# Spectrum by rows: the second transform of a long FFT as two constant 64 by 64 weights, in a kernel that filters and routes tokens

## The chip, the cores and the metric

The kernel runs on one core of a Trainium2 chip. The metric is the device time of one execution in microseconds (us). The kernel before takes 374.61 us, the median of three runs that lie between 374.57 and 374.65 us.

The engines are PE (TensorE matmuls; PEld is its weight load), DVE (VectorE), ACT (ScalarE), POOL (GpSimd) and SP, which here only issues DMAs. Matmul results land in PSUM; only DVE and ACT read it in this kernel.

## The reference

The input `x` is (8, 2496, 256) in fp32: 8 batches of 2496 tokens of 256 channels. Per channel a circular convolution runs over the tokens, as an FFT, a product with a filter spectrum and an inverse FFT:

```
X = rfft(x, axis=1);  Y = X * (filt_r + 1j * filt_i);  y = irfft(Y)         # (8, 2496, 256)
logits = y @ phi                                   # all 19968 tokens, 32 slots
d = softmax(logits over tokens);   slot_in  = d.T @ y                        # (32, 256)
slot_out = relu(slot_in @ w1[e]) @ w2[e]           # 8 experts with 4 slots each
c = softmax(logits over slots);    out = c @ slot_out
```

The output is (19968, 256) in fp32.

## The kernel before, in words

2496 is 39 times 64, which have no common factor, so a token has two indices (`s` below 39, `k` below 64) and the transform is one over 39 followed by one over 64. Since the input is real, 20 frequencies `t` of the first transform are kept. The filtered tokens are never formed: logits and the weighted sum over tokens are both taken in the spectrum.

**Batches and slots.** A batch has 10 slots of two `t` each; the main loop runs over 80 slots, `n` = 0 to 79. The first transform of batch `b+1` is made while batch `b` goes through its slots, in six units `u` of 512 elements a partition (the one with `u` = 0 has half).

**A unit of the first transform.** SP loads `xt` from HBM (`load_x`, six buffers). `fold_x` adds and subtracts the tokens `s` and 39-`s`: two ops on POOL (lines L334 and L337). `s1_unit` (L355) makes four matmuls of 64 rows by 64 columns, one on each quarter of PE, 512 columns wide, with the constant `w1q`. ACT copies the result to `at` (L364), and `store_a` stores it to the HBM scratch `a_dram`. `load_ash` reads it back with the 64 `k` (real and imaginary part) on the 128 partitions. Batch 0 has a way of its own (`first_stage`, `turn`) and is not stored.

**A slot.** `x_unit` (L433) makes the second transform with the DATA as weights: four matmuls with 128x128 blocks of `ash` as weights and 128 columns of a constant as the moving operand. Out comes the spectrum with channels on partitions and frequencies along the row, in `ps_x`, a PSUM pool of two buffers of one bank. DVE multiplies it by the filter: `t2` = spectrum (parts swapped) times the filter's imaginary part (L453), spectrum times the real part in place (L455), one sum and one difference into `yt` (L456, L457). From batch 6 on (`PA`) the last two run on POOL. `t_unit` (L465) transposes `yt` (four 128x128), and ACT copies this to `y`, frequencies on partitions, which is kept for the weighted sum. Every second slot `l_unit` (L492) multiplies `phi` with `yt`: the logits' spectrum.

**The chains.** When a group of batches (two, two, two, one, one) is through its slots, its `chain` takes the logits' spectrum back to tokens (`ltr`, `v`, `lg`), takes the maximum and the exponential (`d`), transforms that (`u`, `u2`, `dd`) and sums `dd` times `y` (`s`). A chain is a generator in steps; two steps go into each slot (`hop_slot`). DVE makes its PSUM copies, maxima and differences.

**After the loop** come the last chain steps, the experts, and the output (`combine`, `blocks`: L1100, L1105), stored through `ob`.

**What sets the order.** Each engine works in order through a list that the framework makes: it simulates the program and lets each engine take the instruction that is ready first and of the highest priority. Chosen edges without a wait (`not_before`, `behind`) fix PE's order in a slot and all early DMA issues on SP. So the order of a list may differ from that of the source, and a wait for a semaphore holds up everything behind it on its engine.

Of the kernel before, what the change touches and what calls it, by code (L numbers as in the profile page):

```python
# [205 lines left out]
def token_layout(x):  # L206

    rows = np.zeros((len(x), 2, 64, NH, 2, DIM), x.dtype)
    for u in range(NH):
        for k in range(PK * 2 * u, min(PK * 2 * (u + 1), N2)):  # L210
            r, j = divmod(k - PK * 2 * u, PK)
            for s in range(HR):
                rows[:, r, HR * j + s, u, 0] = x[:, token_of(s, k)]
                if s:
                    rows[:, r, HR * j + s, u, 1] = x[:, token_of(N1 - s, k)]
    return rows.reshape(len(x), P, NI, DIM)
# [36 lines left out]
def fft_soft_moe(ctx, tc, x0, w0, x, ff, phi, wx, cst, w1q, sgn, out):  # L253
# [73 lines left out]
    def fold_x(b, u):  # L327

        lo, hi = PIECE[u]
        n = hi - lo  # L330
# [3 lines left out]
        ins = eng.tensor_tensor(out=eo[:, 0, 0:n], in0=xs[:, :, 0], in1=xs[:, :, 1], op=ALU.add)  # L334
# [2 lines left out]
        ins = eng.tensor_tensor(out=eo[:, 1, 0:n], in0=xs[:, :, 0], in1=xs[:, :, 1], op=ALU.subtract)  # L337
# [6 lines left out]
    def s1_unit(b, u, floor=None):  # L344
        if u == 0:
            a_dram[b] = scr.tile([2, N2, NT, DIM], F32, tag="a_dram", name=f"a_dram{b}")
        lo, hi = PIECE[u]
        n = hi - lo
        eo = eos.pop((b, u))
        both = ps_s1[0].tile([P, 2, 2, DIM], F32, tag="s1", name=f"s1_{b}_{u}")  # L350
        with tc.high_priority():
            for c, r in ((1, 0), (1, 1), (0, 0), (0, 1)):
                q = slice(64 * r, 64 * r + 64)
                ps = both[64 * c : 64 * c + 64, r, 0:n]
                ins = pe.matmul(ps, w1q_t[q, c], eo[q, c, 0:n], start=True, stop=True)  # L355
# [8 lines left out]
        act.copy(at[:, 0:n], both[:, :, 0:n].rearrange("q r u d -> q u r d"))  # L364
# [25 lines left out]
    def load_ash(b, c):  # L390
        t0 = 2 * c
        ash = prod.tile([P, 2, DIM], F32, tag="ash", name=f"ash{b}_{c}", bufs=ASH)
        ashs[b, c] = ash
        issue(ash, a_dram[b].rearrange("r k t d -> (r k) t d")[:, t0 : t0 + 2, :])
# [756 lines left out]
```

## Time and profile before

| | |
|---|---|
| median of three runs | 374.61 us |
| the profiled execution's own time | 377.61 us |
| its span, first to last instruction | 375.8 us |
| PE busy | 345.0 us, 92% of the span |
| DVE busy | 262.4 us, 70% |
| ACT busy | 175.8 us, 47% |
| POOL busy | 149.1 us, 40% |
| bytes moved by DMA | 104.17 MB, mean 277 GB/s |
| granted TensorE clock, mean | 0.951 |
| main loop (slots 0 to 79) | 16.9 to about 276 us of the span |

The stretch up to 16.9 us loads the first tokens and makes batch 0's first transform; that behind 276 us holds the last chain steps, the experts (about 302 to 319 us) and the output. The profile's page gives shares over the whole span; its view by windows cuts these into stages, and a restriction to one line (L433) shows where a batch begins, since each batch has 80 instructions of that line (each fp32 matmul is two).

### The profile page before, as it was taken

Reading aid. Unit: us, or ns where it says so; the run is one execution under the profiler, and the core shown is the slowest. Engines: PE = TensorE matmul, PEld = TensorE weight load, DVE = VectorE, ACT = ScalarE, POOL = GpSimd, SP = SyncE. Lnnn points to the kernel's source line nnn. Section 1 sums busy time; section 2 is a strip of 40 time slices with the busy share of each in tenths; the row PEclk is TensorE's granted clock in tenths of the full one; section 3 lists DMA queues with packets and bytes.
Section 4 is the critical chain, followed back from the end, with each engine's and each line's share of the span. In section 5 each row is a group of like instructions: output and inputs, shape, how many; then the busy total and the mean of one; then the engine's idle time right before and its main releaser. Section 6 shows DMA issues by size and latency. Waiting matters only on the chain. (4 is left out here: it accounts for less than half of the span.)

```text
span 375.8 us, 10512 instructions
## 1 busy us (share of the span) xinstructions
PE 345.0 (92%) x4254; PEld 257.5 (69%) x4254; DVE 262.4 (70%) x519; ACT 175.8 (47%) x354; POOL 149.1 (40%) x180
## 2 busy tenths in 40 slices
PE   8998989899998899999889998899989999999960
PEld 6865767578676567777566775777867635879960
DVE  2555878796998869689996857685674552786650
ACT  3474545445556244646534544534363430765540
POOL 0189638536348204644640664333531302650000
PEclk9999999999999999999999999999999999995555
DMA  8999899699699549969953757642897993599996
GB/s 301 396 394 352 246 332 360 213 335 384 216 367 337 175 110 317 323 211 297 320 176 102 200 167 219 248 139 60 271 364 227 363 298 82 238 415 413 415 419 285
DMA packets 50438, 104.17 MB, mean 277 GB/s; under 512 B 5250, under 2 KB 23810, under 8 KB 48214
## 3 DMA queue, kind: packets, MB, share of 16 engines
q1 hardware_dynamic: 49700, 103.16, 78.8%
q8 instruction: 33, 0.54, 0.6%
q10 hardware_dynamic: 690, 0.35, 0.3%
q14 instruction: 15, 0.12, 0.1%
HBM read 63.37 MB, written 40.12 MB: 275 GB/s over the span
## 5 line engine op out<-in xcount | busy, mean ns | idle before, releaser
L433 PE MATMUL x<-cst_t,ash 128*128 128x128 f32 x640 | 85.7, 276 | 3.1 <-DMA ash<-a_dram 3.1
L453 DVE TENSOR_TENSOR t<-x,ff_t 128x512 f32<-128x512 f32 x80 | 55.2, 690 | 45.2 <-PE x L433 29.4
L334 POOL TENSOR_TENSOR eo<-xt 128x512 f32<-128x512 f32 (+1 forms) x40 | 49.0, 1225 | 94.4 <-issue 86.4
L433 PEld LDWEIGHTS x<-cst_t,ash 128*128 128x128 f32 x640 | 78.1, 192 | 5.3 <-DMA ash<-a_dram 3.8
L364 ACT COPY at<-s 128x1024 f32<-128x1024 f32 (+1 forms) x42 | 39.6, 943 | 50.0 <-PE s L355 33.2
L465 PE MATMUL t<-cst_t,yt 128*128 128x128 f32 x320 | 49.9, 278 | 0.0
L337 POOL TENSOR_TENSOR eo<-xt 128x512 f32<-128x512 f32 (+1 forms) x40 | 48.5, 1212 | 0.0
L479 ACT COPY y<-t 128x512 f32<-128x512 f32 x58 | 33.8, 587 | 30.8 <-PE t L465 30.6
L355 PE MATMUL s<-eo,w1q_t 64*64 64x512 f32 (+1 forms) x336 | 42.8, 579 | 4.6 <-POOL eo L337 4.4
L455 DVE TENSOR_TENSOR x<-x,ff_t 128x512 f32<-128x512 f32 x60 | 41.8, 696 | 1.3
L465 PEld LDWEIGHTS t<-cst_t,yt 128*128 128x128 f32 x320 | 36.0, 141 | 9.5 <-issue 5.6
L1100 PE MATMUL out<-so,st 32*128 32x256 f32 x468 | 36.0, 367 | 1.1 <-DVE ob L1105 0.9
L1100 PEld LDWEIGHTS out<-so,st 32*128 32x128 f32 x468 | 32.7, 253 | 3.6 <-DVE ob L1105 1.7
L492 PEld LDWEIGHTS l<-yt,phi_t 128*32 128x32 f32 x640 | 15.2, 109 | 25.9 <-issue 20.7
L1105 DVE COPY ob<-out 128x512 f32<-128x512 f32 (+1 forms) x40 | 25.2, 672 | 8.5 <-PE out L1100 7.8
L456 POOL TENSOR_TENSOR yt<-yt,t 128x256 f32<-128x256 f32 x20 | 15.1, 754 | 35.0 <-DVE yt L455 25.3
L1105 ACT COPY ob<-out 128x512 f32<-128x512 f32 (+1 forms) x40 | 21.9, 581 | 14.0 <-PE out L1100 11.4
L456 DVE TENSOR_TENSOR yt<-x,t 128x256 f32<-128x256 f32 x60 | 25.2, 421 | 1.3
L492 PE MATMUL l<-yt,phi_t 128*32 128x128 f32 x640 | 25.7, 278 | 0.0
L457 DVE TENSOR_TENSOR yt<-x,t 128x256 f32<-128x256 f32 x60 | 24.9, 415 | 0.0
L526 PE MATMUL s<-y,dd 128*32 128x256 f32 x232 | 19.2, 381 | 0.3 <-ACT dd L680 0.3
L479 ACT COPY yb<-t 128x512 f32<-128x512 f32 x20 | 11.7, 586 | 10.7 <-PE t L465 10.7
(117 smaller groups left out, 481.9 us busy)
## 6 DMA issues: line engine op xcount, KB each, us to landing
xt<-in_x SPq DMA_DIRECT2D x35, 512.0 KB
ash<-a_dram SPq DMA_DIRECT2D x70, 256.0 KB
out<-ob SPq DMA_DIRECT2D x17, 1024.0 KB
a_dram<-at SPq DMA_DIRECT2D x56, 240.0 KB
w<-in_wx SPq DMA_DIRECT2D x33, 256.0 KB
w<-in_wx SPq DMA_DIRECT2D x6, 512.0 KB
x_t<-in_x SPq DMA_DIRECT2D x5, 512.0 KB
ff_t<-in_ff SPq DMA_DIRECT2D x10, 256.0 KB
```

What stands on the lines that cost most here:

```text
L334: ins = eng.tensor_tensor(out=eo[:, 0, 0:n], in0=xs[:, :, 0], in1=xs[:, :, 1], op=ALU.add)
L337: ins = eng.tensor_tensor(out=eo[:, 1, 0:n], in0=xs[:, :, 0], in1=xs[:, :, 1], op=ALU.subtract)
L355: ins = pe.matmul(ps, w1q_t[q, c], eo[q, c, 0:n], start=True, stop=True)
L433: ins = pe.matmul(ps[:, 2 * k + dh].rearrange("q r c -> q (r c)"), ash[:, k, dh * P : (dh + 1) * P], C("a1" if t0 + k else "b0"), start=Tr ...
L453: dve.tensor_tensor(out=t2, in0=ps[:, :, ::-1, :], in1=fiv, op=ALU.mult)
L455: dve.tensor_tensor(out=part, in0=ps, in1=frv, op=ALU.mult)
L456: add.tensor_tensor(out=yt[:, :, 1, :], in0=part[:, :, 1, :], in1=t2[:, :, 1, :], op=ALU.add)
L465: ins = pe.transpose(pt[:, k, dh, :], yt[:, c % 2, 2 * k + dh].rearrange("q r c -> q (r c)"), ident)
L479: act.copy(y, pt.rearrange("k p h d -> k p (h d)"))
L492: ins = pe.matmul(pl[32 * j : 32 * j + 32, :], phi_t[:, dh, :], yt[:, j // 2, 2 * (j % 2) + dh].rearrange("q r c -> q (r c)"), start=(dh = ...
L1100: nc.tensor.matmul(prs[k][:, mm, :], sts[n][q, hs, c0 : c0 + P], so[q, ho], start=(i == 0), stop=(i == 2))
L1105: copy(ob[:, nm * k : nm * (k + 1), :], prs[k])
```

## The change

**The tokens are folded over both indices.** The 64 `k` are folded too: of `k` and 64-`k` the sum and the difference are formed before the first transform. `fold_x` therefore has four ops in place of two: sum and difference over `k` into a scratch tile `eo` (one buffer, `EB`), then sum and difference over `s` back into `xt`. All four have 512 elements a row (256 for `u` = 0). The second of the four runs on DVE (`FD = (1,)`), the others on POOL; for the first two units all run on DVE. `xt` is read by the matmul itself, so it comes free when `s1_unit` is done, not when the fold is done. The load of the next `xt` is issued behind that unit's store (`next_x` in `store_a`).

**The second transform has constant weights.** A slot pair (four `t`) has one `x_pair`: four matmuls of 64 by 64, one on each quarter of PE, 512 columns wide, with the constants `xf` and `xf0` as weights and `ash` as the moving operand (six matmuls for the pair that holds `t` = 0). Batch 0, which is not folded over `k`, has 128 rows by 64 columns. The spectrum stands in rows: frequencies on partitions, channels along the row. That is the layout of `y`, so DVE's product goes to `y` directly, with 1024 and 512 elements an op. `t_pair` then transposes `y` to `yt` for `l_unit`.

**Buffers.** `ps_x` holds one pair (two banks) in one buffer; before it held two slots in one bank each. `ash` has three buffers of a pair (before seven of a slot), `t2` one (before two).

**In the chain** `dd` is made in halves of 64 columns so that its rows match those of `y`. The sign of the imaginary table is a column of the constants (`sgn`), no longer a table of its own.

The first engine shown is DVE, in batch 1. Names: `x_1_2`, `t2_1_2` belong to batch 1 and slot 2 (before) or pair 2 (change); `eo3_5`, `xt3_5` are the fold and the loaded tokens of batch 3, unit 5. What stands in brackets are the semaphores that the instruction waits for (DMAHW: a DMA has landed). Before:

```order
L453 TENSOR_TENSOR t2_1_2_729<-x_1_2_724,ff_t_101 128x512 [waits PE_49]
L455 TENSOR_TENSOR x_1_2_724<-x_1_2_724,ff_t_101 128x512 [waits DVE_49]
L453 TENSOR_TENSOR t2_1_3_753<-x_1_3_748,ff_t_101 128x512 [waits PE_49]
L456 TENSOR_TENSOR yt_1_2_730<-x_1_2_724,t2_1_2_729 128x4x64 [waits DVE_49]
L457 TENSOR_TENSOR yt_1_2_730<-x_1_2_724,t2_1_2_729 128x4x64
L455 TENSOR_TENSOR x_1_3_748<-x_1_3_748,ff_t_101 128x512 [waits DVE_49]
L456 TENSOR_TENSOR yt_1_2_730<-x_1_3_748,t2_1_3_753 128x4x64 [waits DVE_49]
L457 TENSOR_TENSOR yt_1_2_730<-x_1_3_748,t2_1_3_753 128x4x64
```

With the change:

```order
L510 TENSOR_TENSOR t2_1_2_727<-x_1_2_722,ff_t_101 128x1024 [waits DVE_49,PE_49]
L373 TENSOR_TENSOR eo3_4_926<-xt3_4_704 128x512 [waits DMAHW3_49,Pool_49]
L512 TENSOR_TENSOR x_1_2_722<-x_1_2_722,ff_t_101 128x1024 [waits DVE_49]
L513 TENSOR_TENSOR yb_1_0_619<-x_1_2_722,t2_1_2_727 128x512 [waits DVE_49]
L514 TENSOR_TENSOR yb_1_0_619<-x_1_2_722,t2_1_2_727 128x512
L373 TENSOR_TENSOR eo3_5_1030<-xt3_5_761 128x512 [waits DMAHW7_49,Pool_49]
L510 TENSOR_TENSOR t2_1_3_794<-x_1_3_789,ff_t_101 128x1024 [waits DVE_49,PE_49]
```

Folds of batch 3 now stand in DVE's list among the products of batch 1, and each waits for the landing of a load from HBM (DMAHW).

The same place on PE, with the change (before, each slot had its own `t` and `x`, and two slots shared one `l`):

```order
L485 MATMUL x_1_2_722<-ash1_2_644,cst_t_73 64x512 x4
L391 MATMUL s1_2_5_732<-xt2_5_459,w1q_t_72 64x512 x4
L523 MATMUL t_1_1_0_740<-cst_t_73,yb_1_0_619 128x128 x4
L523 MATMUL t_1_1_1_746<-cst_t_73,yb_1_0_619 128x128 x4
L571 MATMUL ltr_1_0_955<-cst_t_73,lt_1_706 128x128
L540 MATMUL l_1_1_763<-yt_1_1_739,phi_t_74 32x128 x8
L391 MATMUL s1_3_0_774<-xt3_0_490,w1q_t_72 64x256 x4
L485 MATMUL x_1_3_789<-ash1_3_695,cst_t_73 64x512 x4
```

The product of pair 1 is transposed behind the second transform of pair 2; and `s1_2_5`, whose end frees the buffer that `xt3_5` is loaded into, stands right behind `x_1_2`.

On SP, where these loads are issued, with the change:

```order
L337 DMA a_dram2_478<-at2_5_737 60x4x256 [waits DMAHW5_49,Activation_49]
L337 DMA a_dram2_478<-at2_5_737 60x4x256 [waits DMAHW6_49]
L337 DMA xt3_5_761<-in_x 128x1024 [waits DMAHW7_49,PE_49,Pool_49]
L337 DMA ash2_0_781<-a_dram2_478 128x1024 [waits DMAHW5_49,DMAHW2_49,DMAHW6_49,DMAHW1_49,DMAHW0_49]
L337 DMA a_dram3_773<-at3_0_779 20x2x256 [waits Activation_49]
```

The load of `xt3_5` comes behind the two stores of `at2_5`. Before, a load waited for POOL's fold alone and was not behind its unit's store.

The diff, cut to its core:

```diff
-XC = 4
+PPB = CPB // 2
 XB = 6
+EB = 1
+FD = (1,)
-ASH = 7
+NA = 3
+T2 = 1
@@ slot_of
-    return CPB * b - 5 - (2 * (NU - 1 - u) if u else CPB + (b > 2))
+    return CPB * b - 6 - (2 * (NU - 1 - u) if u else CPB - 1)
@@ fft_soft_moe
-    ps_x = ctx.enter_context(tc.tile_pool(name="ps_x", bufs=2, space=PSUM))
+    ps_x_cm = tc.tile_pool(name="ps_x", bufs=1, space=PSUM, side="right")
+    ps_x = ps_x_cm.__enter__()
@@ fold_x
-        eng = dve if (b, u) < (1, 2) else pool_e
-        ins = eng.tensor_tensor(out=eo[:, 0, 0:n], in0=xs[:, :, 0], in1=xs[:, :, 1], op=ALU.add)
-        ins = eng.tensor_tensor(out=eo[:, 1, 0:n], in0=xs[:, :, 0], in1=xs[:, :, 1], op=ALU.subtract)
-        eos[b, u] = eo
+        early = (b, u) < (1, 2)
+        for k, (o, i0, i1, op) in enumerate((
+            (sd[:, 0], xs[:, 0], xs[:, 1], ALU.add),
+            (sd[:, 1], xs[:, 0], xs[:, 1], ALU.subtract),
+            (xs[:, 0], sd[:, :, 0], sd[:, :, 1], ALU.add),
+            (xs[:, 1], sd[:, ::-1, 0], sd[:, ::-1, 1], ALU.subtract),
+        )):
+            eng = dve if early or k in FD else pool_e
+            ins = eng.tensor_tensor(out=o, in0=i0, in1=i1, op=op)
+        eos[b, u] = xs
@@ store_a
+            next_x()
@@ split_next
-            next_x()
             fold_x(b, u)
@@ x_unit -> x_pair
-        for k in range(2):
-            for dh in range(2):
-                ins = pe.matmul(ps[:, 2 * k + dh].rearrange("q r c -> q (r c)"),
-                    ash[:, k, dh * P : (dh + 1) * P], C("a1" if t0 + k else "b0"), start=True, stop=True)
+        ps = ps_x.tile([P, 2, 2, DIM], F32, tag="x", name=f"x_{b}_{i}")
+        for r, k in ((0, 0), (0, 1), (1, 0), (1, 1)):
+            for lo, hi in ((0, 1), (1, 2)) if i + k == 0 else ((0, 2),):
+                if b:
+                    rows, w = slice(64 * r, 64 * r + 64), C("xf" if i + k + lo else "xf0")
+                else:
+                    rows, w = slice(0, P), C("a1" if i + k + lo else "b0", 64 * r, 64 * r + 64)
+                ins = pe.matmul(ps[64 * k : 64 * k + 64, r, lo:hi], w[rows], ash[rows, lo:hi, k], start=True, stop=True)
...
+        dve.tensor_tensor(out=t2, in0=ps[:, ::-1], in1=fiv, op=ALU.mult)
+        add, part = (pool_e, y) if b >= PA else (dve, ps)
+        dve.tensor_tensor(out=part, in0=ps, in1=frv, op=ALU.mult)
+        add.tensor_tensor(out=y[:, 1], in0=part[:, 1], in1=t2[:, 1], op=ALU.add)
+        add.tensor_tensor(out=y[:, 0], in0=part[:, 0], in1=t2[:, 0], op=ALU.subtract)
+    def t_pair(b, i):
+        for c in range(2):
+            for r in range(2):
+                for dh in range(2):
+                    ins = pe.transpose(pt[:, dh, r, :], ys[b, 2 * i + c][:, r, dh * P : (dh + 1) * P], ident)
+            act.copy(yt[:, c], pt)
@@ chain, dd
-            pe_m(pd[:, 0:n], C("b1"), u2[:, t0 : t0 + n], start=True, stop=True)
+            for r in range(2):
+                for k in range(2):
+                    o = pd[64 * k : 64 * k + 64, 0 : n // 2, :, r]
+                    pe_m(o, C("b1", 64 * r, 64 * r + 64), u2[:, t0 + k : t0 + n : 2], start=True, stop=True)
@@ main loop
-        if n >= LT:
-            t_unit(*divmod(n - LT, CPB))
-            x_unit(*divmod(n, CPB))
+        if n % 2 == 0 and n < NS:
+            x_pair(*divmod(n // 2, PPB))
+        if n % 2 == 0:
+            for b, u in at_slot.get(n, ()):
+                s1_unit(b, u, held[0])
+        if n % 2 == 0 and n >= LT:
+            t_pair(*divmod(n // 2 - 1, PPB))
...
+        if n % 2:
+            for b, u in at_slot.get(n, ()):
+                s1_unit(b, u, held[2] or held[0])
```

More of the change, by code (lines that the diff above doesn't have):

```diff
@@ L141, in shape_constants @@
     put("id", np.eye(P))
+    put("sgn", sgn.reshape(NT // 2, P).T)
+    xf = np.zeros((2, 2, 2, NK, N2))
+    for r in range(2):
+        for m in range(NK):
+            i = index_of(r, m)
+            if i:
+                xf[0, r, 0, m], xf[0, r, 1, m] = co[i], si[i]
+                xf[1, r, 0, m], xf[1, r, 1, m] = -si[i], co[i]
+            else:
+                even = np.arange(N2) % 2 == 0
+                xf[0, r, 0, m], xf[0, r, 1, m] = even, ~even
+                xf[1, r, 0, m], xf[1, r, 1, m] = ~even, even
+    xf0 = xf.copy()
+    xf0[..., N2 // 2 + 1 :] = 0
     put("m0", inverse(bh))
@@ L206, in token_layout @@
 def token_layout(x):
[L208 to L216, printed above, removed]
+    n = len(x)
+    part = np.zeros((n, 2, 64, 2, 2, P), x.dtype)
+    full = np.zeros((n, 2, 64, NU - 1, 2, 2, DIM), x.dtype)
+    for r in range(2):
+        for m in range(NK):
+            k = index_of(r, m)
+            for kk, i in enumerate((k, N2 - k if k else N2 // 2)):
+                for s in range(HR):
+                    for a, n1 in enumerate((s, N1 - s) if s else (0,)):
+                        v = x[:, token_of(n1, i)]
+                        if m < NJ:
+                            full[:, r, HR * (m % PK) + s, m // PK, kk, a] = v
+                        else:
+                            part[:, :, HR * r + s, kk, a] = v.reshape(n, 2, P)
+    rows = np.concatenate([part.reshape(n, P, -1), full.reshape(n, P, -1)], axis=2)
+    return rows.reshape(n, P, NI, DIM)
 def first_layout(x):
@@ L388, in fft_soft_moe, with load_ash @@
     ashs = {}
[L390 to L394, printed above, removed]
+    def load_ash(b, i):
+        ash = prod.tile([P, 4, DIM], F32, tag="ash", name=f"ash{b}_{i}", bufs=NA)
+        ashs[b, i] = ash
+        issue(ash, a_dram[b][:, 4 * i : 4 * i + 4, :])
     def first_stage(u):
@@ L482, in l_unit @@
-    def l_unit(b, c):
-        yt = yts[b, c // 2]
-        i = c // 2
+            ff_t[:, 2 * i : 2 * i + 2, k].rearrange("q (o c) d -> q o c d", o=1).broadcast_to([P, 2, 2, DIM])
+            for k in range(2)
+        )
+        t2 = prod.tile([P, 2, 2, DIM], F32, tag="t2", name=f"t2_{b}_{i}", bufs=T2)
+        k = (b * CPB + 2 * i) % YB - CPB
+        if 0 <= k < CPB:
+            if k == 0 and b * CPB + 2 * i < NS - CPB:
+                big[0] = ypool.tile([P, PPB, 2, 2, DIM], F32, tag="yb", name=f"yb_{b}_{i}", bufs=1)
+            y = big[0][:, k // 2]
+        else:
+            y = ypool.tile([P, 2, 2, DIM], F32, tag="y", name=f"y_{b}_{i}")
@@ L502, in l_unit @@
         held[2] = ins
-        act.copy(lts[b][:, i, :], pl)
+        act.copy(lts[b][:, i, :], pl.rearrange("q r c -> q (r c)"))
     c_dram = {}
```

246 lines of the change are left out of this document (116 added, 130 removed), and 4 rows, old and new, of the table TAIL.

## The prediction

> **What bounds the kernel now.** I first read the view by windows, cut at the batches. Restricted to the line of the second transform (L433) it counts 80 to 82 instructions a window, which fixes the cuts:
>
> ```profile
> 47.40:74.60 27.20, 10.90 (x80) 9.66 (x80) 1.00 0.88 305
> 242.90:276.50 33.60, 10.82 (x80) 9.67 (x80) 1.00 0.55 178
> ```
>
> The same windows for all engines (length, then PE, PEld, DVE, ACT and POOL busy with their counts, granted clock, DMA share, GB/s), batch 0 to 7:
>
> ```profile
> 16.90:47.40 30.50, 28.39 (x284) 19.95 (x280) 20.09 (x39) 17.18 (x29) 24.79 (x25) 1.00 0.96 332
> 47.40:74.60 27.20, 24.13 (x255) 17.16 (x253) 21.82 (x44) 13.14 (x24) 15.50 (x14) 1.00 0.88 305
> 74.60:103.90 29.30, 29.29 (x347) 21.64 (x348) 23.87 (x47) 14.49 (x25) 12.97 (x12) 1.00 0.91 310
> 103.90:142.30 38.40, 35.97 (x461) 25.55 (x460) 32.16 (x61) 18.62 (x36) 14.73 (x13) 1.00 0.73 250
> 142.30:171.80 29.50, 29.50 (x353) 21.85 (x351) 25.02 (x50) 15.08 (x26) 14.07 (x13) 1.00 0.87 282
> 171.80:210.10 38.30, 35.88 (x460) 25.46 (x459) 33.54 (x64) 18.84 (x37) 14.70 (x13) 1.00 0.69 219
> 210.10:242.90 32.80, 30.24 (x396) 23.48 (x395) 22.09 (x39) 16.04 (x32) 17.25 (x22) 1.00 0.68 216
> 242.90:276.50 33.60, 33.25 (x443) 26.19 (x442) 24.07 (x43) 12.81 (x28) 14.16 (x21) 1.00 0.55 178
> ```
>
> PE is the bound: in batches 0 to 5 it is busy for 183.2 of 193.2 us, 94.8%. But DVE comes close behind, at 21.8 to 33.5 us a batch. So PE time that is saved pays only down to what DVE needs. DVE's products, their share of it, are in the view by lines:
>
> ```profile
> L453 DVE TENSOR_TENSOR t<-x,ff_t 128x512 f32<-128x512 f32 x80 | 55.2, 690 | 45.2 <-PE x L433 29.4
> ```
>
> **What PE saves.** Two slots' second transform, and the form that the change gives it, which the first transform has already (timeline: start, length, line, count):
>
> ```profile
> 44.19 1.06 PE L433 MATMUL x<-cst_t,ash 128*128 128x128 f32 x8
> 45.17 1.09 PE L355 MATMUL s<-eo,w1q_t 64*64 64x512 f32 x8
> 46.19 0.64 PE L492 MATMUL l<-yt,phi_t 128*32 128x128 f32 x16
> ```
>
> Eight instructions of L355 at 615 ns each (rows below) would take 4.9 us one after the other; they take 1.09, so the quarters do run at once. By starts, a slot takes 45.17 - 44.19 = 0.98 us and a unit 46.19 - 45.17 = 1.02. A pair falls from 1.96 to 1.02 us; I allow 0.1 for the pair with six matmuls and take 0.84 us, 4.2 us a batch in batches 1 to 7. Batch 0 has 128 rows by 64 columns; nothing shows that form. Below stands a unit's 1.02 us a pair, above four matmuls in a row (4.9). L492, 128 rows by 32 columns, does overlap (16 instructions of 278 ns in 0.64 us), so I take two halves at once: no gain. The same holds for `dd`: nothing, at worst its busy time once more:
>
> ```profile
> L355 PE MATMUL s<-eo,w1q_t 64*64 64x512 f32 x280 | 38.1, 614 | 4.6 <-POOL eo L337 4.4 <-ACT at L364 0.2
> L526 PE MATMUL dd<-u,cst_t 128*128 128x512 f32 (+4 forms) x36 | 11.6, 449 | 0.6 <-DVE u L672 0.6
> ```
>
> Transposes, logits, and ACT's copies keep their number and size.
>
> **What DVE gains and gets.** Its products before, and the fold ops:
>
> ```profile
> L455 DVE TENSOR_TENSOR x<-x,ff_t 128x512 f32<-128x512 f32 x60 | 41.8, 696 | 1.3
> L456 DVE TENSOR_TENSOR yt<-x,t 128x256 f32<-128x256 f32 x60 | 25.2, 421 | 1.3
> L457 DVE TENSOR_TENSOR yt<-x,t 128x256 f32<-128x256 f32 x60 | 24.9, 415 | 0.0
> L337 POOL TENSOR_TENSOR eo<-xt 128x512 f32<-128x512 f32 x34 | 44.1, 1296 | 0.0
> L334 DVE TENSOR_TENSOR eo<-xt 128x512 f32<-128x512 f32 x1 | 0.7, 687 | 0.0
> L632 DVE TENSOR_TENSOR d<-lg,m_run 117x512 f32<-117x512 f32 x6 | 6.1, 1052 | 0.3
> ```
>
> A pair costs 2 x (690 + 696 + 421 + 415) = 4444 ns now. From 256 to 512 elements an op grows by 690 - 421 = 269 ns, so one of 1024 costs 690 + 2 x 269 = 1228; two of them and two of 512 make 3.84 us. That is 0.6 us less a pair, 3.0 a batch. The new fold op reads two SBUF tiles, and POOL starts its own fold op on the same landing. Alone it costs 687 ns (L334 on DVE). Beside a POOL fold the nearest op, `d`, cost 1052, and POOL's op grew too:
>
> ```profile
> 111.96 1.28 POOL L334 TENSOR_TENSOR eo<-xt 128x512 f32<-128x512 f32 x1 [3.05 <-issue]
> 114.94 1.81 POOL L334 TENSOR_TENSOR eo<-xt 128x512 f32<-128x512 f32 x1 [0.47 <-POOL eo L337]
> 113.76 3.40 DVE L632 TENSOR_TENSOR d<-lg,m_run 117x512 f32<-117x512 f32 x3
> ```
>
> Bounds 0.69 and 1.05; I take 1.05 (0.6 for the half unit): 5.85 us a batch. POOL gets three ops of 1.3 us a unit, some 21 us a batch, and stays below the batch.
>
> **The single buffer.** `x_pair` may start when DVE has done the pair before. So DVE sits through each second transform (1.1 us with its handoffs, 5.5 us a batch) unless its list has work between the last difference and the next product. In batch 1 it has two folds and a copy (2.3 us, 3.2 left); in batches 2 to 5 folds and chain work fill four of five places (1.1 left). DVE's need, batch by batch, is its busy time, less 3.0, plus 5.85 (batch 5: 4.2, four folds), plus what is left: batch 1, 27.8 us; 2, 27.8; 3, 36.1; 4, 29.0; 5, 35.8. Batch 0 has 12 folds (11.7 us), 2.2 of extra early ops and 3.5 of uncovered transforms less its saving: about 32.3 us. Together 188.8. At the 94.8% that the bounding engine reaches today that is 199.2 us against 193.2: **6.0 us more**. In batches 6 and 7 the sum and difference run on POOL, no fold is left, PE bounds, and 4.2 us each come off: **8.4 us less**. So far the change is worth -2.4 us.
>
> **What the moved folds wait for.** `eo3_5` on DVE needs `xt3_5`, whose buffer comes free only when `s1_2_5` is done; and that stands directly behind `x_1_2`, whose product DVE has just begun. The way from there:
>
> ```profile
> 71.67 1.02 ACT L364 COPY at<-s 128x1024 f32<-128x1024 f32 x1 [1.40 <-PE s L355]
> 46.62 0.92 SPq L306 DMA_DIRECT2D a_dram<-at  x2
> 71.96 2.71 SPq L306 DMA_DIRECT2D ash<-a_dram  x6
> 74.61 1.16 PE L433 MATMUL x<-cst_t,ash 128*128 128x128 f32 x8 [1.79 <-DMA ash<-a_dram]
> 7.93 0.33 SPq L306 DMA_DIRECT2D ff_t<-in_ff  x1
> 13.57 0.42 DVE L772 TENSOR_TENSOR ff_t<-ff_t,sg 128x256 f32<-128x256 f32 x1 [0.89 <-DMA ff_t<-in_ff]
> ```
>
> 0.1 us to ACT, its copy 1.02, two store issues 0.92, then the load: from issue to use 74.61 - 71.96 = 2.65 us after a pause of the queue, 13.57 - 7.93 = 5.64 us in the crowded start. Sum 4.7 to 7.7 us; the loop's DMA share of 0.7 to 0.9 lies between, I take 6.05. The unit ends 1.0 us behind `x_1_2`. So the fold ends 1.0 + 6.05 + 1.05 = 8.1 us behind it. Without the wait the next product would start after 3.84 + 1.05 (the fold inside the pair) + 1.1 = 6.0 us. DVE stands still for 2.1 us. Behind the waiting fold stands `t2` of the next pair, behind that, by the single buffer, `x_pair` on PE: nothing covers it. The list has seven folds directly behind the product of the pair whose unit frees their buffer, each with another fold inside: 3_5, 4_3, 4_5, 5_3, 6_3, 6_5, 7_3. **7 x 2.1 = 14.7 us more** (0.75 us each by the short way: 5.2; 3.75 by the long one: 26.3). Folds one pair later are reached 1 us behind their load or sooner; I leave them in the 5.2% of idle time.
>
> Sum: -2.4 + 14.7 = +12.3 us. Against the profiled execution's 377.6 us that is 389.9. The median of the runs is 3.0 us below that execution, so I forecast **387 us**, slower.
>
> The Trainium skill, "DMA: Bandwidth & Descriptors", Specifications, gives some 0.6 us to the first byte of such a DMA and 435 GB/s; estimated from that page alone a 512 KB load would land in 1.8 us, and the fold's wait would vanish. No landing here was that short: 2.65 us for half the bytes. The time by that rule is the first rival's.
>
> **The rivals.**
>
> *The loads land in time: faster.* DVE's list was made so that nothing waits in the simulated program; if the real pairs are longer, or the way of a load shorter, the 14.7 us vanish, and the sum is -2.4 us (372); with folds at 0.69 us (1.8 us a batch less) and DVE as dense as PE was in batches 2 and 4 (100%) it reaches 362. For it speaks that PE waits little on DMA today; against it that before no DVE product stood behind a load. 33%, about 368 us.
>
> *Nothing to tell:* wait and gain cancel, within 0.2% (0.75 us, about what a measurement of this kernel can tell from no change). 5%.
>
> *PE's clock falls.* With DVE as bound PE is busy 20 of some 32 us in batch 1, and the last stage shows what a less busy PE gets:
>
> ```profile
> 340.00:376.00 36.00, 23.41 (x253) 22.29 (x248) 15.75 (x27) 13.36 (x27) 0.00 (x0) 0.50 0.92 380
> ```
>
> At half the clock batch 1's 20 us of PE become 40, those of batches 2 and 4 (25 us) 50: 40 us more, 425 us. Against it: no stage of the loop was below 1.00. 4%. The Trainium skill, "TensorE: Matmul & The Clock Gate", Part 1, ties the fall to an idle window of about 3.4 us; by that rule PE's gaps of 2 to 3 us here would leave it at full speed.
>
> *The quarters do not overlap:* excluded by L355's rows above.
>
> **How the numbers follow.** Forecast 58%, clock 4%, faster 33%, same 5%. Slower holds 62%. The forecast's own range, by the short and the long way of a load, is 374.6 - 2.4 + 5.2 = 377 to 374.6 - 2.4 + 26.3 = 398, with 4 us for batch 0's unseen form and `dd`: 402. Since a third lies with the faster case, the range for 8 in 10 reaches from 363 to 402.
>
> **What would show it.** In the changed profile: batches 6 and 7 shorter by some 4 us each (PE's saving real); L510 at about 1.23 us, the DVE rows of L373 near 1.05; batches 1, 2 and 4 longer than 27.2, 29.3 and 29.5; DVE idle ahead of L373 by some 2 us at the seven folds, ended by a DMA; PE busy below 85% in batches 1, 2 and 4. I am wrong if DVE has no idle time ahead of L373, or if batches 2 and 4 get shorter.

## The result and the profile after

The changed kernel takes **435.32 us** (median of 4 runs, 433.83 to 440.24), the kernel before 374.63 us beside it: a ratio of 1.164 with a 95% interval of 1.155 to 1.173. The forecast was 387 us with a range of 363 to 402. The sign was right; the loss is 57.0 us of span (432.8 against 375.8), where the sum gave 12.3.

The view by windows, cut where a batch begins (length, then PE, PEld, DVE, ACT and POOL busy, granted clock, DMA share, GB/s), batch 0 to 7 and the rest:

```profile
16.80:67.60 50.80, 35.08 (x243) 14.98 (x239) 27.78 (x34) 17.89 (x30) 48.95 (x40) 0.90 0.73 236
67.60:103.30 35.70, 24.01 (x217) 11.27 (x217) 23.45 (x29) 12.01 (x21) 27.74 (x23) 0.90 0.82 256
103.30:143.80 40.50, 31.22 (x316) 16.25 (x316) 26.77 (x38) 14.43 (x26) 23.30 (x19) 0.89 0.68 204
143.80:189.70 45.90, 37.62 (x446) 21.23 (x442) 34.12 (x44) 18.26 (x36) 22.62 (x19) 0.88 0.61 175
189.70:227.40 37.70, 30.05 (x314) 15.99 (x314) 26.48 (x37) 14.42 (x26) 23.88 (x19) 0.90 0.75 229
227.40:267.70 40.30, 35.92 (x448) 20.43 (x444) 33.95 (x46) 18.33 (x37) 17.56 (x13) 0.92 0.63 189
267.70:295.90 28.20, 26.17 (x290) 14.63 (x290) 16.51 (x20) 12.71 (x24) 11.69 (x10) 1.00 0.74 234
295.90:330.40 34.50, 33.04 (x474) 20.88 (x473) 23.13 (x34) 13.68 (x31) 10.83 (x9) 1.00 0.58 195
330.40:432.80 102.40, 84.94 (x1217) 62.89 (x1215) 55.22 (x125) 44.34 (x109) 21.84 (x50) 0.86 0.79 304
```

Batch 7 is cut at the end of its last product into `t2`, in both kernels, so it has 32.9 us before and the rest 100.0. The differences are +20.3 us in batch 0, +8.5, +11.2, +7.5, +8.2 and +2.0 in batches 1 to 5, -4.6 in batch 6, +1.6 in batch 7 and +2.4 behind it. In batches 1 to 5 no engine is full: POOL has 28 of 36 us in batch 1, DVE 23, PE 24. In batch 0 POOL is busy for 49 of 51 us.

What DVE waits for in batches 1 to 5, from the view of the waits (us in total, times, longest):

```profile
DVE eo L373 <- DMA xt<-in_x: 38.5, 16, 5.4
DVE t L510 <- PE x L485: 11.7, 11, 2.1
DVE eo L373 <- POOL xt L373: 2.8, 4, 1.3
```

Sixteen folds wait for a load, 2.4 us in the mean (0.65 to 5.37). One of them in the chain of waits (start, length, what):

```profile
78.86 6.08 DMA xt<-in_x
...
85.04 0.69 DVE eo L373
85.73 1.16 DVE x L512
...
88.25 1.98 PE x L485 x8
```

The same fold and the next one in the timeline, with the unit that frees the next one's buffer and the issue of its load on SP:

```profile
81.54 1.04 PE L391 MATMUL s<-xt,w1q_t 64*64 64x512 f32 x8
84.62 0.72 SPq L337 DMA_DIRECT2D xt<-in_x  x1
...
85.04 0.69 DVE L373 TENSOR_TENSOR eo<-xt 128x512 f32<-128x512 f32 x1 [2.02 <-DMA xt<-in_x]
...
89.99 0.69 DVE L373 TENSOR_TENSOR eo<-xt 128x512 f32<-128x512 f32 x1 [1.79 <-DMA xt<-in_x]
```

The first load takes 6.08 us from issue to landing. Its fold stands between the two products of a pair, so it holds `x` in the only buffer of `ps_x`, and the next second transform starts some 2 us late, at half speed (1.98 us, with a granted clock of 0.50 from 88.20 to 90.20 us; it takes 1.09 at a clock of 1.00). By the lists above the fold at 85.04 us is `eo3_4` and that at 89.99 us `eo3_5`; every sixth fold has 256 elements a row, so all of them can be numbered in this way.

In batch 0 the same folds wait for something else. DVE rows, then POOL rows, then the second transform that they hold up:

```profile
32.41 0.69 DVE L373 TENSOR_TENSOR eo<-xt 128x512 f32<-128x512 f32 x1 [1.37 <-POOL xt L373]
36.83 0.69 DVE L373 TENSOR_TENSOR eo<-xt 128x512 f32<-128x512 f32 x1 [3.73 <-POOL xt L373]
41.27 0.42 DVE L373 TENSOR_TENSOR eo<-xt 128x256 f32<-128x256 f32 x1 [3.75 <-POOL xt L373]
...
44.42 1.22 DVE L510 TENSOR_TENSOR t<-x,ff_t 128x1024 f32<-128x1024 f32 x1
...
36.88 1.78 POOL L373 TENSOR_TENSOR eo<-xt 128x512 f32<-128x512 f32 x1
38.73 2.50 POOL L373 TENSOR_TENSOR xt<-eo 128x512 f32<-128x512 f32 x2
...
51.44 3.68 PE L485 MATMUL x<-ash,cst_t 128*64 128x512 f32 x8 [5.69 <-DVE y L514]
```

A unit takes POOL 36.83 - 32.41 = 4.4 us, and by the single `eo` DVE's fold waits for POOL's last op of the unit before. The second transform at 51.44 us comes after 5.7 us in which PE had nothing to do. L373 alone in the window of batch 0 (length, DVE and POOL busy with their counts, granted clock, DMA share, GB/s):

```profile
16.80:67.60 50.80, 9.43 (x14) 41.36 (x32) 0.90 0.73 236
```

POOL has 32 fold ops there, 41.4 us.

### The profile page after: what moved, and what is told of

The parts are those of the page before. It is cut to its first block, busy times and chain, and to the rows that moved or that the text cites. A ratio compares the mean times of both kernels' runs of the same rounds, so it can differ in the third digit from the quotient of the medians.

```text
span 432.8 us, 10012 instructions
## 1 busy us (share of the span) xinstructions
PE 352.8 (82%) x4054; PEld 211.2 (49%) x4054; DVE 274.1 (63%) x423; ACT 172.5 (40%) x354; POOL 208.8 (48%) x200
## 4 chain that ended last, share of the span: by engine, by line
PE 32%; DMA 20%; DVE 19%; POOL 12%; issue 5%; ACT 5%; SPq 2%; ACTq 0%; DVEq 0%; POOLq 0%
DMA xt<-in_x 14%; POOL xt L373 7%; PE x L485 5%; PE s L391 4%; DVE t L510 3%; DVE x L512 3%; PE out L1148 3%; DMA out<-ob 3%; POOL eo L373 3%; PE v L574 2%; ACT at L407 2%; SPq L337 2%; PE dd L574 2%; DMA phi_t<-in_phi 2%; PE s L574 2%
## 5 line engine op out<-in xcount | busy, mean ns | idle before, releaser
L373 POOL TENSOR_TENSOR xt<-eo 128x512 f32<-128x512 f32 (+1 forms) x80 | 93.6, 1191 | 11.1 <-DVE eo L373 3.2
L373 POOL TENSOR_TENSOR eo<-xt 128x512 f32<-128x512 f32 (+1 forms) x40 | 62.9, 1571 | 65.7 <-DMA xt<-in_x 64.4
L485 PE MATMUL x<-ash,cst_t 64*64 64x512 f32 (+3 forms) x352 | 58.7, 656 | 32.8 <-DVE y L514 18.2
L510 DVE TENSOR_TENSOR t<-x,ff_t 128x1024 f32<-128x1024 f32 x40 | 48.9, 1221 | 33.0 <-PE x L485 21.1
L373 DVE TENSOR_TENSOR eo<-xt 128x512 f32<-128x512 f32 (+1 forms) x44 | 29.0, 663 | 60.0 <-DMA xt<-in_x 38.5
L391 PE MATMUL s<-xt,w1q_t 64*64 64x512 f32 (+1 forms) x336 | 49.9, 666 | 5.0 <-POOL xt L373 5.0
L529 ACT COPY yt<-t 128x512 f32<-128x512 f32 x80 | 43.5, 594 | 17.6 <-PE t L523 17.4
L540 PE MATMUL l<-yt,phi_t 128*32 128x128 f32 x640 | 37.3, 286 | 9.1 <-ACT yt L529 7.3
L523 PEld LDWEIGHTS t<-cst_t,y 128*128 128x128 f32 x232 | 26.6, 147 | 25.4 <-issue 18.1
L485 PEld LDWEIGHTS x<-ash,cst_t 64*64 64x64 f32 (+1 forms) x352 | 14.3, 145 | 48.6 <-DVE y L514 21.9
L1148 PE MATMUL out<-so,st 32*128 32x256 f32 x468 | 35.5, 337 | 2.0 <-ACT ob L1153 1.0
L512 DVE TENSOR_TENSOR x<-x,ff_t 128x1024 f32<-128x1024 f32 x30 | 36.8, 1227 | 0.5
L513 POOL TENSOR_TENSOR y<-y,t 128x512 f32<-128x512 f32 x9 | 11.5, 1274 | 48.5 <-DVE y L512 44.4
L523 PE MATMUL t<-cst_t,y 128*128 128x128 f32 x232 | 34.5, 289 | 0.2
L540 PEld LDWEIGHTS l<-yt,phi_t 128*32 128x32 f32 x640 | 19.2, 110 | 23.8 <-ACT yt L529 21.6
```

What stands on the lines that cost most here:

```text
L373: ins = eng.tensor_tensor(out=o, in0=i0, in1=i1, op=op)
L391: ins = pe.matmul(bf[64 * c : 64 * c + 64, r], w1q_t[q, c], eo[q, c].rearrange("q f d -> q (f d)"), start=True, stop=True,)
L485: ins = pe.matmul(ps[64 * k : 64 * k + 64, r, lo:hi], w[rows], ash[rows, lo:hi, k], start=True, stop=True)
L510: dve.tensor_tensor(out=t2, in0=ps[:, ::-1], in1=fiv, op=ALU.mult)
L512: dve.tensor_tensor(out=part, in0=ps, in1=frv, op=ALU.mult)
L523: ins = pe.transpose(pt[:, dh, r, :], ys[b, 2 * i + c][:, r, dh * P : (dh + 1) * P], ident)
```

## The experiments

Each edit is on the changed kernel unless the sentence ahead of it names another. For each stand its median, that of the kernel before on the same chip, and their ratio with its 95% interval.

### Folds held back

```diff
-FD = (1,)
+FD, LEAD = (1,), 3
@@ fold_x
-            if early:
-                not_before(ins, held[4])
+            if early or b > 2:
+                not_before(ins, held[4 if early else 5])
@@ split_next
-        for b, u in at_slot.get(n, ()):
+        for b, u in [p for m, f in ((n, 0), (n - 1 + LEAD, 1)) for p in at_slot.get(m, ()) if (p[0] > 2) == f]:
```

> Edit: the folds of batches 3 to 7 are written three slots ahead of their unit in place of one, and each may be taken into an engine's list only behind the last x or t matmuls that are written before it (an edge without a wait). So DVE's list no longer holds folds a whole batch ahead. The work is the same. Theory A (the time goes to DVE's folds that stand ahead of products and wait for their load): the 38.5 us that DVE sat idle ahead of L373 until a DMA are gone; batches 1 to 5, 200.1 us now, fall to about 165, the whole to about 400 us; batch 0 keeps its 50.8 us. Rival B (POOL's three ops a unit set the pace, and the loads are only what is seen last): batches 1 to 5 stay above 190 us and the whole above 425. Rival C (the granted clock of 0.9 in batches 0 to 5 is the cause): no change either, above 425, since the edit does not touch PE's work.

Measured: 392.21 us against 376.85, ratio 1.041 (1.030 to 1.052). DVE's waits in batches 1 to 5 and batches 1 and 5 of the windows:

```profile
DVE t L510 <- PE x L485: 6.4, 10, 1.1
DVE eo L373 <- POOL xt L373: 5.7, 4, 1.6
```
```profile
67.40:94.50 27.10, 21.48 (x222) 10.49 (x220) 24.18 (x29) 12.13 (x22) 21.60 (x18) 1.00 0.82 254
189.60:225.40 35.80, 32.58 (x442) 19.41 (x442) 33.79 (x48) 18.08 (x37) 22.04 (x19) 1.00 0.74 232
```

No fold waits for a load any more, and batches 1 to 5 take 158.0 us in place of 200.1: 42 us come back with the same work, in another order. Batch 0 keeps 49.4 us. The granted clock in these batches goes from 0.9 to 1.00, so the low clock was a consequence of the waits, not the cause (rival C falls, and B for these batches). Part of the 42 us may have run through it, as in the transform of 1.98 us above.

### Folds all on POOL; half of the fold left out; two buffers for `eo`

```diff
-FD = (1,)
+FD = ()
```

> Edit: all four ops of a fold go to POOL (the first two units stay on DVE). DVE waits for no load and for no fold any more, and POOL gets a fourth op of some 1.27 us a unit, about 5.1 us a unit and 28 us a batch of 5.5 units. Theory A (DVE's folds hold up the products): batches 1 to 5 fall from 200.1 us to about 165, batch 0 to 36 to 40 us, because only four units of batch 1 and the tables (28 us of POOL) are needed in it; the whole about 385 to 390 us. Rival B (POOL sets the pace): batch 0 holds ten units, 51 us and 8 us of tables, and gets no shorter than the 50.8 us of now; the whole above 430 us.

Measured: 396.46 us against 376.85 (1.053, 1.041 to 1.064). Batches 1 to 5 fall to 166.3 us, as theory A has it; batch 0 takes 46.3, far more than the 36 to 40 expected. PE's `s1` now waits for POOL, for 6.4 us ahead of one unit of batch 0 and 1.9 ahead of another.

```diff
-        )):
+        )[0:2]):
             eng = dve if early or k in FD else pool_e
```

> Left out: the second pair of a fold's four ops (over s), so the first transform reads the raw tokens and the output is not the reference's. DVE keeps its one op a unit with all its waits, POOL has one op a unit in place of three, and xt still comes free only behind the unit's matmuls. Theory A: the waits for loads (38.5 us) stay, the waits of DVE for POOL (21.2 us, nearly all in batch 0 and the start of batch 1) go: batch 0 falls from 50.8 to about 33 us, batches 1 to 5 lose 5 us or less, the whole about 408 to 415 us. Rival B (POOL sets the pace everywhere): batches 1 to 5 fall to about 160 us too and the whole to about 375.

Measured: 425.68 us against 376.85 (1.130, 1.118 to 1.142). Batches 1 to 5 take 200.8 us, as in the changed kernel, though POOL has a third of its ops: its pace isn't what holds these batches. Batch 0 falls to 41.3 us, not to 33: DVE's folds wait for loads 24 times in all, in place of 16.

```diff
-EB = 1
+EB = 2
```

> Edit: the scratch tile eo gets a second buffer. DVE's fold no longer waits for POOL's last two ops of the unit before, but for those of the unit before that. If the single buffer as such is what DVE waits for in batch 0 (21.2 us in all): batch 0 falls by some 15 us and the whole to about 415 us. Theory A with POOL as the pace of batch 0 (4.4 us a unit): DVE's folds run one unit ahead and then wait as long for POOL as before; batch 0 falls by 5 us or less, and the whole stays within 425 to 433 us.

Measured: 450.28 us against 376.85 (1.196, 1.181 to 1.210), slower than either guess. Batch 0 keeps 48.6 us, so the single buffer as such is not its cause; batches 1 to 5 grow to 217.1. With the second buffer the fold ops of DVE meet those of POOL at other places: L373 on DVE takes 1171 ns in the mean in place of 663. e11 shows such meetings one by one.

### Batch 0

On e1_late_folds:

```diff
-FD, LEAD = (1,), 3
+FD, LEAD = (1,), 2
-            if early or b > 2:
+            if early or b > 1:
```

and the same bound in `split_next`.

> Edit: as in e1_late_folds, but from batch 2 on and two slots ahead in place of three, so that the folds of batch 2, which stand in batch 0, are held back as well. POOL's work in batch 0 stays. If batch 0's 49.4 us (in e1_late_folds) come from DVE's list alone (folds of batch 2 ahead of the products of batch 0): batch 0 falls to 35 us or less and the whole from 392 to about 378. If POOL's pace of 4.4 us a unit and its 8 us of tables hold up PE's s1 (POOL was busy 49 of 50.8 us): batch 0 stays above 45 us and the whole between 388 and 394.

Measured: 391.20 us against 376.05 (1.040, 1.037 to 1.043); batch 0 49.3 us. The order of the later folds isn't what holds batch 0.

On e1_late_folds:

```diff
-        early = (b, u) < (1, 2)
+        early = b == 1
```

> Edit: e1_late_folds, and all folds of batch 1 (six units, the first two already) run on DVE, four ops of 0.69 us each. POOL then has three and a half units fewer in batch 0, some 15 us, and DVE three more ops in each of four units, 12 x 0.69 = 8.3 us. If POOL sets batch 0's pace: batch 0 falls from 49.4 to about 36 us (five products of 3.84, six folds of 2.8 us and little more on DVE), and the whole from 392 to about 379. If the crowded loads at the start set it (a load of xt lands 12 to 16 us behind its issue there): batch 0 stays above 45 us.

Measured: 383.86 us against 376.05 (1.021, 1.017 to 1.024). Batch 0 falls to 40.2 us: 9 us of it were POOL's pace. It stays 9.7 us longer than before. Some 4.0 of these are batch 2's folds: e14, which leaves them out, takes 36.1 us there, and e8, which is the same otherwise, 40.1. What holds the other 5.6 us was not tried apart.

### Sums on DVE in batches 6 and 7, and the edits together

On e1_late_folds:

```diff
-PA = 6
+PA = 8
```

> Edit: e1_late_folds, and the sum and difference of the products stay on DVE in batches 6 and 7 (PA = 8 in place of 6). In batch 7 the starts of L510 lie 5.03 us apart (281.66, 286.69 us), which is 1.23 + 1.23 on DVE and 1.27 + 1.27 on POOL one after the other: the single t2 keeps the next pair waiting for POOL. Theory: that loop holds batch 7, whose 33.0 us are no shorter than the 32.9 of before; with both on DVE a pair needs 3.84 us, batch 7 falls by 2 to 4 us, batch 6 by up to 2, the whole to 387 to 390 us. Rival: PE bounds batches 6 and 7 (29.6 of 31 us busy there), and DVE gets 5.5 us more in each: no change, 391 to 394 us.

Measured: 392.43 us against 376.05 (1.044, 1.040 to 1.047). Batch 6 falls from 29.5 to 27.4 us, batch 7 rises from 33.0 to 34.5: nothing is won in sum, as the rival said, but neither batch stays as it was. POOL's sums are not what holds batch 7.

> The edits of e1_late_folds, e6_batch1_on_dve and e7_sums_on_dve together. If their gains add: about 392 - 13 - 3 = 376 us, within 1% of the kernel before. If batch 0 is held by its loads: about 388 us.

Measured: 380.97 us against 376.05, 1.013 (1.011 to 1.016): the gains do not add to the 376 expected. It is the fastest version that computes the whole result, and it is slower than the kernel before.

On e1_late_folds with `PA` = 8:

```diff
-            eng = dve if early or k in FD else pool_e
+            eng = dve if early or k in ((1, 3) if b == 1 else () if b in (5, 7) or u % 2 == 0 else FD) else pool_e
```

> Edit: late folds and sums on DVE as in e8_three_edits; batch 1's units 2 to 5 have two ops on DVE and two on POOL (all four on DVE in e8_three_edits); of the later batches the units with even number and all units of batches 5 and 7 (which are folded while a chain fills batches 3 and 5) have no op on DVE, the rest keep one. Theory (in batches 1 to 5 DVE is the bound once its waits are gone, in batch 0 DVE and then POOL): batch 0 falls from 40.1 to about 35 us, batches 1, 2 and 4 by about 1 us each, batches 3 and 5 (35.5 and 35.8 us) by 2 to 3 us each; the whole from 381 to about 368, 2% faster than the kernel before. Rival (PE with the single ps_x bounds these batches, or POOL's extra op at 1.27 us holds up s1): batches 1 to 5 stay within 1 us each, the whole about 376 us.

Measured: 383.03 us against 375.56 (1.021, 1.018 to 1.024). The theory fell: batches 2 and 4 stay at 29.7 and 29.6 us although DVE has 1.5 and 2.4 us less to do, batches 3 and 5 win 1.0 and 1.2 us in place of 2 to 3, batch 0 only 0.8, and batch 1 grows from 27.4 to 32.1 us, with POOL busy for 31.0 of them. In batches 2 and 4 DVE's busy time is not the bound.

Likewise on e1_late_folds with `PA` = 8:

```diff
-            eng = dve if early or k in FD else pool_e
+            eng = dve if early or k in ((1, 3) if b == 1 else ()) else pool_e
```

> As e9_shared_folds, but from batch 2 on no unit has an op on DVE: POOL needs 5.1 us a unit, 28 us for the 5.5 units of a batch. If POOL becomes the bound there: batches 1, 2 and 4 take 28.5 us as in e2_all_on_pool, batches 3 and 5 about 33; the whole 1 to 3 us above e9_shared_folds, about 370 us. If DVE's ops are what costs: 1 to 3 us below it.

Measured: 384.88 us against 375.56 (1.023, 1.018 to 1.027). Batches 2 and 4 take 28.6 and 28.5 us, as expected with POOL as the bound, but e14 takes 28.6 us there with POOL idle: POOL isn't what holds them. Batches 3 and 5 take 38.4 and 37.9 us in place of 33, with POOL busy for 37.2 and 33.7.

### The single buffer of `ps_x`

On e8_three_edits:

```diff
-        add, part = (pool_e, y) if b >= PA else (dve, ps)
+        add, part = dve, y
```

> Edit on e8_three_edits: the second product of a pair is written to y in place of ps_x, so the single ps_x comes free two ops (1.36 us) earlier; every engine keeps its ops. In e9_shared_folds batch 4 pairs followed each other with DVE busy 24.1 and PE 27.2 of 29.6 us, neither full. Theory (the single buffer sets the pace: x_pair 1.1 us, then four DVE ops of 3.84, then the next x_pair, 5.05 us a pair): a pair's loop falls to 1.1 + 2.45 us and DVE's own work sets the pace; batches 1, 2 and 4 (27.4, 29.8, 29.8 us) fall by 1 to 3 us each, the whole from 381 to about 371 us. Rival (PE's list with its waits for ACT's copies sets the pace): less than 3 us in all.

Measured: 403.90 us against 375.13 (1.075, 1.071 to 1.080), the opposite of what was expected. DVE no longer waits for `x` in batch 1, but its own ops grow. Three DVE ops of one pair, and what POOL does meanwhile:

```profile
62.53 1.30 DVE L373 TENSOR_TENSOR eo<-xt 128x512 f32<-128x512 f32 x1
63.76 0.68 DVE L513 TENSOR_TENSOR yb<-yb,t 128x512 f32<-128x512 f32 x1
64.36 1.75 DVE L514 TENSOR_TENSOR yb<-yb,t 128x512 f32<-128x512 f32 x1
```
```profile
62.02 1.27 POOL L373 TENSOR_TENSOR eo<-xt 128x512 f32<-128x512 f32 x1
63.98 3.27 POOL L373 TENSOR_TENSOR xt<-eo 128x512 f32<-128x512 f32 x2 [0.69 <-DVE eo L373]
```

L513 and L514 are the same op; with both operands in SBUF one takes 0.68 us and the next, which runs wholly beside POOL's ops, 1.75; POOL's two ops take 3.27 us in place of 2.50. In the kernels where one operand comes from `ps_x`, L513 and L514 take 0.69 and 0.68 us beside the same POOL ops.

On e8_three_edits, `l_unit` one slot later, with `t_pair` where it was:

```diff
-LT = 2
+LT = 3
-        if n % 2 == 0 and n >= LT:
+        if n % 2 == 0 and 2 <= n <= NS:
             t_pair(*divmod(n // 2 - 1, PPB))
```

> Edit on e8_three_edits: the logits' matmuls of a pair (L540) are written one slot later, behind the transposes of the next pair. Now they stand directly behind their own transposes, wait 0.5 us for ACT's first copy and again inside the group (1.12 us in place of the 0.65 us of before), some 1 us of PE a pair. If PE's list sets the pace: up to 1 us a pair of batches 1 to 7, the whole from 381 to about 360 to 370 us. If the single ps_x with DVE's products sets it: under 3 us in all.

Measured: 394.19 us against 375.13 (1.049, 1.044 to 1.055), slower too, though L540's group does fall from 1.12 to 0.64 us. `LT` also sets the slot in which a chain starts, so the chains start one slot later too. PE idles longer before the second transform, and the clock falls. Windows around one such gap in batch 1:

```profile
67.70:69.00 1.30, 0.00 (x0) 0.00 (x0) 1.27 (x3) 0.27 (x1) 1.30 (x2) 1.00 0.93 234
69.00:72.60 3.60, 3.52 (x16) 0.81 (x16) 3.34 (x5) 0.00 (x0) 2.80 (x4) 0.53 0.92 305
```

Batch 1 has a granted clock of 0.84 in all. The clock is 1.00 in batches 3 to 6, which are longer too; what costs them time there isn't settled.

> The edits of e11_free_ps_x and e12_l_later together. If the single ps_x is the bound and PE's list stands right behind it: more than the sum of the two gains, the whole about 362 to 368 us, 2 to 3% faster than the kernel before. If DVE's own work (26.2 of 29.8 us in batch 2) is the next bound: about 370 us.

Measured: 424.32 us against 375.13 (1.133, 1.123 to 1.142), the opposite of what was expected: the two losses add and more. To see `ps_x` without collisions, the folds were left out from batch 2 on, in e8_three_edits, in e11_free_ps_x and in e13_both:

```diff
-        for k, (o, i0, i1, op) in enumerate((
+        for k, (o, i0, i1, op) in enumerate(() if b > 1 else (
```

> Left out, on e8_three_edits: all folds from batch 2 on, so the first transform reads the raw tokens there and the output is not the reference's. POOL is idle in batches 1 to 7 and DVE has its products and the chains alone. The single ps_x stays. In e8_three_edits pairs follow each other at 5.03 us in batch 1 (L510 at 70.24, 75.31, 80.33, 85.38 us), with DVE idle 0.6 us ahead of each L510 until x_pair. Theory (x_pair and DVE's four products take turns on the single ps_x): pairs stay at about 5.0 us, batches 2 and 4 at 28 to 29.8 us, batch 1 at 26 to 27. Rival (the fold ops on DVE and their collisions with POOL set the pace): pairs fall to about 4.4 us, batches 1, 2 and 4 by 3 us each.

> As e14_no_folds (the same work left out), with the second product written to y, so ps_x is free two ops earlier; there is no POOL op for DVE's SBUF ops to meet, and L514 should take 0.68 us again in place of 1.75 in e11_free_ps_x. Theory: the turns end, and PE's list sets the pace (x 1.1, s1 1.0, t 1.1, a wait of 0.5, l 1.1): 4.7 to 4.8 us a pair, batches 1, 2 and 4 shorter by 1 to 2 us each than in e14_no_folds. Rival (ps_x is not the bound): no change.

> As e15_no_folds_free (the same work left out), with the logits' matmuls one slot later as in e12_l_later. Theory: PE's list loses its wait inside l, DVE's 3.8 us of products bound a pair: 3.9 to 4.4 us a pair, batches 1, 2 and 4 shorter by 2 to 4 us each than in e15_no_folds_free. If the granted clock falls where PE idles, as it did in batch 1 of e12_l_later (0.84), part of that is lost.

Two products of `t2` in a row in batch 1, in e14, in e15 and in e16:

```profile
75.44 1.22 DVE L510 TENSOR_TENSOR t<-x,ff_t 128x1024 f32<-128x1024 f32 x1 [1.21 <-PE x L485]
80.49 1.23 DVE L510 TENSOR_TENSOR t<-x,ff_t 128x1024 f32<-128x1024 f32 x1 [1.23 <-PE x L485]
```
```profile
74.24 1.22 DVE L510 TENSOR_TENSOR t<-x,ff_t 128x1024 f32<-128x1024 f32 x1 [1.34 <-PE x L485]
78.89 1.23 DVE L510 TENSOR_TENSOR t<-x,ff_t 128x1024 f32<-128x1024 f32 x1 [0.97 <-PE x L485]
```
```profile
71.18 1.22 DVE L510 TENSOR_TENSOR t<-x,ff_t 128x1024 f32<-128x1024 f32 x1 [0.86 <-PE x L485]
75.35 1.23 DVE L510 TENSOR_TENSOR t<-x,ff_t 128x1024 f32<-128x1024 f32 x1 [0.48 <-PE x L485]
```

e14: 373.35 us against 376.22 (0.994, 0.990 to 0.998). A pair of batch 1 takes 5.05 us with no fold at all, as the theory had it: the second transform and DVE's four products in turns on one buffer. The whole fold, on both engines, costs e8 only 2.1 us in batch 1 and 1.2 us in batches 2 and 4 (27.4, 29.8 and 29.8 against 25.3, 28.6 and 28.6); that is short of the rival's 3 us each, though in batch 1 more than the theory's 26 to 27 us left room for.

e15: 366.40 us (0.973, 0.969 to 0.977). L514 takes 0.68 us again, and a pair of batch 1 takes 4.65 us: PE's list, with its wait for ACT's copy inside, has no other gap left. Batch 1 falls by 1.3 us, but batches 2 and 4 only by 0.5 each, less than the 1 to 2 expected: with a chain's steps in them PE was busy for 26.8 of 28.6 us in e14 already. Batches 3 and 5 fall by 1.0 us each, batch 7 by 2.8 (34.6 to 31.8); yet in e11, by the same edit, batch 7 stays at the 33.8 us of e8, so what holds it remains open.

e16: 366.79 us (0.974, 0.959 to 0.990; its two runs, 364.46 and 369.12, lie too far apart to tell it from e15). A pair takes 4.17 us, batches 1, 2 and 4 fall to 21.6, 25.1 and 24.5, while batches 3, 5 and 7 are longer than in e15 (35.5, 35.9 and 36.2 us against 34.2, 34.2 and 31.8).

So in batch 1 the turns on `ps_x` are the bound behind the waits, as the theory of e11 had it, with PE's list 0.4 us a pair behind them; in batches 2 and 4 that list stands closer still. And even with no fold from batch 2 on, e8 is only 0.6% faster than the kernel before.

## Why the prediction was right in sign and wrong in size

| part of the span | forecast | measured |
|---|---|---|
| waits of folds for loads | 14.7 us, 7 x 2.1 | 42.1 us (changed kernel less e1, batches 1 to 5); 38.5 us, 16 x 2.4, as DVE's idle time |
| batches 1 to 5 without these waits | 165.1 us (156.5 by 94.8%) | 158.0 us in e1 |
| batch 0 | 34.1 us (32.3 by 94.8%) | 50.8 us |
| batch 6, batch 7 | -4.2 us each | -4.6 and +1.6 us |
| behind the loop | none | +2.4 us |

**The mechanism of the waits was right; the count was wrong, and the price came out near by luck.** Of the seven folds that the forecast names, six waited: 18.1 us in all, 3.0 in the mean, where 7 x 2.1 = 14.7 were taken; 6_5 found its load landed. But **ten more waited**, 2.0 us in the mean and 20.4 in all. So the step that failed is "Folds one pair later are reached 1 us behind their load or sooner; I leave them in the 5.2% of idle time." The fold at 85.04 us in the rows above, `eo3_4`, is one of these ten: its load is issued at 78.86 us and takes 6.08, and DVE waits 2.02 us for it.

The price of a wait was too low because the load was. For `eo3_5` the forecast took 6.05 us from the end of its unit to its use; the rows have 82.58 (81.54 + 1.04) to 89.99 us, 7.41. The part up to the issue was right (2.04 us in both), the load took 5.4 us in place of 4.0. That this fold waited for only 1.79 us is because DVE came to it late, after the wait of `eo3_4` in the same pair; without that wait it would have been some 3.8 (an estimate, 1.79 + 2.02). Nor does such a list recover: the second transform that starts late at 88.25 us has its unit behind it, at 90.56 us, the next load is issued behind that unit's store, at 94.58 us, and the fold that needs it, at 100.10 us, waits 2.30 us again.

**Batch 0 was mis-sized by 16.7 us.** The failed step is "POOL gets three ops of 1.3 us a unit, some 21 us a batch, and stays below the batch." That is the mean batch. The forecast counts 12 folds in batch 0 itself and charged them to DVE alone; POOL has 32 of its ops there, 41.4 us, and its tables, and is full. e6 gave back 9.2 us by taking four units from POOL. A slip of the sum is in it too: DVE's 20.1 us and the terms named, 11.7 + 2.2 + 3.5 - 3.0, make 34.5 us, not 32.3; the 2.2 us of early ops were not added.

**DVE as the bound of batches 1 to 5 gave nearly the right time for a reason that is only partly right.** The terms "DVE's need" of batches 1 to 5 (27.8, 27.8, 36.1, 29.0, 35.8) stand against 27.1, 29.8, 35.4, 29.9 and 35.8 us in e1; with the 94.8% on top they are 7 us too long in sum. But e9 and e10 took DVE's fold ops away and won little. What sets a pair of batch 1 is the turn of x_pair and four products, 5.05 us, which the forecast had as an addition to DVE's work ("DVE sits through each second transform", 1.1 us with its handoffs): right as a price, and shown by e14 and e15. In batches 2 and 4 the turns are worth only 0.5 us (e15), because PE's list, which the forecast did not take as a bound there, stands right behind them.

**Single prices.** L510 took 1.22 us (forecast 1.23). The fold op on DVE takes 0.69 us, not 1.05; it is POOL's first op that grows, from 1.27 to 1.78 us. The Trainium skill, "SBUF — State Buffer", SBUF: two separate sides, says that a DVE op with two SBUF inputs and a GpSimd op that reads SBUF lock each other out of a shared pair of ports, first come, first served; 1.78 against 1.27 alone beside a DVE op of 0.69, and 1.75 against 0.68 for L514 in e11, agree with it. A second transform in quarters took 1.09 us, as forecast; in batch 0's form 1.94 us, two halves at once, also as forecast. Logits were taken to keep their cost, and did not: L540's group takes 1.12 us, 0.65 before, because it waits for ACT's copy inside.

**The rivals.** The loads did not land in time. The clock's fall was given 4%, and the Trainium skill's rule ("TensorE: Matmul & The Clock Gate", Part 1, an idle window of some 3.4 us) stood against it; the clock fell to 0.9 in batches 0 to 5, and in e12 to 0.53 behind a gap of 1.3 us. No gap of 3.4 us was needed: the transform at 88.25 us, at 0.50, stands behind one of 2.33. But not every such gap lowers it: the transform at 74.87 us takes 1.09 us behind one of 2.52, so these traces show no threshold. As a cause of the loss in batches 1 to 5 it is excluded by e1, where they run at 1.00.

**The signs named beforehand.** DVE idle ahead of L373 by about 2 us, ended by a DMA: yes. PE below 85% in batches 1, 2 and 4: 67, 77 and 80%. Batches 1, 2 and 4 longer: yes. Batches 6 and 7 shorter by 4 us each: only batch 6. In batch 7 PE stays busy for 33.0 of 34.5 us: its second transform does need less, but more steps of a chain lie in it (264 matmuls of `u` from there to the end in e1, 200 before). This, and the 2.4 us behind the loop, stay open.

## What to carry to other kernels

An op moved onto an engine that works in order brings its wait along: ask for every one of them what it waits for on its new engine and what stands behind it, and count all of them, not those that wait longest on paper. Sum each engine over the stage with the most work, not over the mean stage. And where a buffer is made single, the two engines that share it take turns: a pair then costs at least the sum of both (here 1.1 + 3.84 us and the handoffs, 5.05), even if each engine alone would need less.

## What the runs showed of the hardware

A DVE op on two SBUF operands and a POOL op hold each other up: 128x512 in fp32 takes 0.68 us on DVE alone and up to 1.76 beside POOL (L514 in e11), while the same op with one operand in PSUM keeps 0.67 to 0.68 us in all 39 cases of e8. So writing an intermediate to SBUF to free PSUM earlier cost some 23 us here (e11 against e8); without POOL's folds the same edit won 7 us (e15 against e14). And PE's granted clock fell to about half behind gaps of 1.3 us (e12) and 2.3 us (changed kernel), while behind another gap of 2.5 us in the changed kernel a second transform ran at full speed.
